# Merged row loads, sums and output stores, and tokens stored in pieces, in an attention kernel with a SwiGLU gate

## Chip, cores and metric

The kernel runs on one core of a Trainium2 chip. The metric is device time in microseconds (us): 1722.99 us, the median of 3 runs (1722.92 to 1723.66). Five engines work side by side, each through its own list of instructions in order: TensorE (PE) for matrix products, VectorE (DVE), ScalarE (ACT), GpSimd (POOL), and SyncE (SP), which here only issues transfers (DMAs). ACT issues a few transfers too. Products land in PSUM, where this kernel has seven banks for them and one for the accumulated attention output.

## What is computed

For 2048 tokens of width 512, in float32:

```python
xn = layernorm(x)
q, k, v = split(xn @ wqkv)          # 32 heads of width 16
p = softmax(q @ k.T * 16 ** -0.5)   # per head, 2048 x 2048
s = (p @ v) @ wo
g = silu((silu(xn @ w1) * (xn @ w3)) @ w2)   # inner width 1792
return x + s * g
```

## The kernel before

**Precision.** Each operand of a product is split into a high and a low part, and three products (low x high, high x low, high x high) give the result. For the 16 rows of one head's keys and queries the three are done in one product over 48 rows: a tile `ks` holds key rows high, low, high, and a tile `qs` query rows high, high, low, 64 rows apart for the two heads of a pair, with two more rows below for the maxima of the softmax.

**First part** (lines 449 to 682). Tokens are loaded in 16 tiles of 128 (`load_x`), normalized, transposed by PE, and split into `xts[b]`, four blocks of 512 tokens. A list `plan` (line 648) then orders the work in steps. Each step makes one product of 12 matmuls: key rows ("k"), query rows ("q") or values ("v") of one block. Then it issues some matmuls of maxima (`max_unit`, line 411: 128 queries against 512 keys of the first pair of heads, reduced by DVE), transposes more token tiles, and last calls a few functions. Keys, queries and values are stored to DRAM (`qk_d`, `v_d`), since later parts read them in another layout: `keep_rows` (line 616) stores one block of key or query rows from SP in two stores (high and low part); `load_k` and `load_q` (lines 392 and 400) bring the 16 rows of a head back, three loads for each of two heads. `keep_tokens` (line 620) stores a block of split tokens from ACT, two stores of 1 MB, for the gate to read later. `token_values` (line 540) copies a value tile on ACT (line 557), stores it from ACT's queue (line 558), and copies a part of it again (line 559). `max_rows` (line 424) turns the maxima of a phase into two rows in `qs`, stored by four small transfers from SP (line 446). `weights_first` starts the loads and splits of the weights for the main part.

**Main part.** 32 phases, one for each half of the queries of 16 pairs of heads. A string, ORDER_OF_ISSUE, gives PE's order letter by letter: "s" a score matmul (`scores`, line 695), followed by an exponential on ACT (line 698); "m" a maximum matmul of the next phase (line 419); "v" four matmuls of probabilities and values (line 711); "f" a matmul of the gate or of the projection of further keys and queries (line 1012). Small and capital letter stand for the two halves of PE's rows. A timing model in the program decides when the work that is not in the string is issued: row loads (`open_chunk`, line 1272), the weights, and the steps of taking out a phase's output, with 16, 1.5, 9, 16 and 5 us between them (LATER).

**Taking out** (`take_out`, line 714). ACT copies the accumulated output `ot`. Four transfers bring the sums of the exponentials into a tile (line 723), DVE takes the reciprocals, one transfer writes them to DRAM (line 727), four read them back broadcast to the rows (line 730). POOL multiplies and splits the result into `oh` and `ol`, and eight transfers store these (line 747). Later `fetch` (line 1047) reads them for the output projection.

**Rows for later heads.** `projected` (line 800) copies a product on ACT, POOL splits it into `ch` and `c`, and SP stores both (line 815). The buffers are shared with those of the gate: ACT's copy to `g` (line 835) reuses one of the two that `ch` uses.

All transfers of one queue leave in the program's order; a transfer that has to wait holds those behind it.

Of the kernel before, what the change touches and what calls it, by code (L numbers as in the profile page):

```python
# [12 lines left out]
ALU = mybir.AluOpType  # L13
# [138 lines left out]
def kernel(ctx: ExitStack, tc: tile.TileContext, x, wqkv, wo, w1, w3, w2, out):  # L152
# [32 lines left out]
    qk_d = [[dram.tile([P, S], F32R, name=f"qk{b}{s}") for s in range(2)] for b in range(8)]  # L185
    o_d = [[[dram.tile([P, 512], F32R, name=f"o{b}{s}{t}") for t in range(TB)] for s in range(2)] for b in range(KC)]
# [204 lines left out]

    def load_k(p, cols=slice(0, S)):
        t = ks[p % 2]
        for h in range(2):
            r = (p % 4) * 32 + h * DH
            kh, kl = (raw(v)[r:r + DH, cols] for v in qk_d[4 + p // 4])
            for n, src in enumerate((kh, kl, kh)):
                nc.sync.dma_start(raw(t)[64 * h + n * DH:64 * h + (n + 1) * DH, cols], src)

    def load_q(p, half, c=None):  # L400
        t = qs[p % 2]
        c = c or slice(half * 1024, (half + 1) * 1024)
        for h in range(2):
            r = (p % 4) * 32 + h * DH
            qh, ql = (raw(v)[r:r + DH, c] for v in qk_d[p // 4])
            for n, src in enumerate((qh, qh, ql)):
                nc.sync.dma_start(raw(t)[64 * h + n * DH:64 * h + (n + 1) * DH, c], src)
# [16 lines left out]
    def max_rows(p, half):  # L424
# [18 lines left out]
        for h in range(2):  # L443
            for n, v in enumerate((mh, ml)):
                r = 64 * h + KM + n
                nc.sync.dma_start(raw(qs[p % 2])[r:r + 1, c], raw(v)[8 * h:8 * h + 8, :])


    with tc.tile_pool(name="pro", bufs=1) as pro, tc.tile_pool(name="pros", bufs=1) as pros:
# [90 lines left out]
        def token_values(b, i):  # L540
# [16 lines left out]
            nc.scalar.copy(vrow[t % 4][:, :, 0:DH], v)  # L557
            nc.scalar.dma_start(v_d[t], vrow[t % 4].rearrange("p h d -> p (h d)"))
            nc.scalar.copy(vt[0][:, t, :, 0:DH], v[:, 0:GH, :])

        nc.gpsimd.memset(raw(ks[0]), 1.0)
        blank = iter([(raw(t), 0.0) for t in qs] + [(r, 1.0) for r in (raw(ks[1]), rb)])
# [35 lines left out]
        first_rows = max_rows(0, 0)  # L598
# [17 lines left out]
        def keep_rows(b, c):  # L616
            for s, st in enumerate(made_rows.pop((b, c))):
                nc.sync.dma_start(raw(qk_d[KC * c][s])[:, b * 512:(b + 1) * 512], raw(st))

        def keep_tokens(b):  # L620
            for s in range(2):
                nc.scalar.dma_start(raw(xt_d[b][s]), raw(xts[b][s]).rearrange("p k t -> p (k t)"))
# [21 lines left out]
        def weights_first():  # L644
            wts.pump(KC)
            wts.fill()

        plan = [
            ("k", 0, (4, 5), 0, keys_here(0)[:1]),
            ("q", 0, (6,), 0, ()),  # L650
            ("v", 0, (7,), 0, queries_here(0)[:1] + keys_here(0)[1:] + queries_here(0)[1:]),
            ("v", 1, (8,), 0, (lambda: keep_tokens(0),)),
            ("k", 1, (9, 10), 0, ()),
            ("q", 1, (11,), 4, keys_here(1)),
            ("v", 2, (12, 13), 5, queries_here(1) + (lambda: keep_tokens(1),)),
            ("k", 2, (14,), 5, ()),
            ("q", 2, (15,), 5, keys_here(2)),
            ("v", 3, (), 6, queries_here(2)),
            ("v", 0, (), 6, (blank_next,)),
            ("k", 3, (), 6, (lambda: load_q(1, 0), lambda: keep_tokens(2))),  # L660
            ("q", 3, (), 6, keys_here(3)),
            ("v", 1, (), 6, queries_here(3) + (lambda: load_q(0, 1),)),
            ("v", 2, (), 6, (blank_next, blank_next, wts.start)),
            ("v", 3, (), 6, (weights_first,)),
            ("v", 0, (), 3, (lambda: next(first_rows), lambda: next(first_rows))),
            ("v", 1, (), 0, (lambda: next(first_rows), lambda: next(first_rows, None))),
            ("v", 2, (), 0, ()),
            ("v", 3, (), 0, ()),
        ]
        done = 0  # L670
        for what, n, tiles_, maxima_, then in plan:
# [9 lines left out]
            for e in then:  # L681
                e()

# [30 lines left out]
    def take_out(p, half):  # L714
# [7 lines left out]
        for j in range(4):  # L722
            nc.sync.dma_start(sums[32 * j:32 * j + 32, :], ot[32 * j + DH:32 * j + VW, :])
# [9 lines left out]
        oh = work.tile([P, 512], F32R, tag="oh", name="oh", bufs=1)  # L733
        ol = work.tile([P, 512], F32R, tag="ol", name="ol", bufs=1)
        nc.gpsimd.tensor_scalar(oh, ot, 1.0, 1.0, op0=ALU.mult, op1=ALU.mult)
        nc.gpsimd.tensor_sub(ol, ot, raw(oh))
        yield
        store_rows(p, half, oh, ol)

    def store_rows(p, half, oh, ol):  # L740
# [764 lines left out]
```

## Time and profile before

| | |
|---|---|
| median of 3 runs | 1722.99 us |
| the profiled execution | 1721.93 us, its span 1719.8 us |
| PE busy | 1699.1 us (99%) |
| DVE, ACT, POOL busy | 80%, 72%, 51% |
| mean granted PE clock | 0.996 |
| transfers | 181.07 MB, 105 GB/s on average |

The profile is of one execution. A row of the timeline reads: start in us, length in us, engine (with a q for its queue of transfers), line, operation, output tile <- input tiles, shape, count, and in square brackets the engine's idle time before it with what ended that. A row of the windows reads: stretch, its length, the busy time of PE, PEld (weight loads of PE), DVE, ACT and POOL with counts, granted clock, share of the 16 DMA engines that was busy, and GB/s. A row of the chain of waits: start, length, what was waited for. Matmuls are pipelined and their ends are modelled.

### The profile page before, as it was taken

How to read it: one execution, taken by the hardware profiler on the slowest of the kernel's cores; microseconds unless marked ns; L12 is line 12 of the kernel's file. 1: busy time of each engine (PE TensorE's matmuls, PEld its weight loads, DVE VectorE, ACT ScalarE, POOL GpSimd, SP SyncE). 2: the span in 40 equal slices, each digit the busy share in tenths (PEclk: the TensorE clock that was granted, in tenths of full speed). 3: DMA queues.
4: the chain of work that ended last, by engine and by line, in shares of the span. 5: the costliest groups of instructions: out<-in, count | busy, mean ns of one | idle time of the engine just before them, and what ended most of it. 6: DMA issues, size and time to landing. Idle time of an engine off the chain costs nothing.

```text
span 1719.8 us, 35915 instructions
## 1 busy us (share of the span) xinstructions
PE 1699.1 (99%) x13476; PEld 1128.0 (66%) x13476; DVE 1371.2 (80%) x2288; ACT 1232.1 (72%) x2449; POOL 877.9 (51%) x926
## 2 busy tenths in 40 slices
PE   9899999999999999999999999999999999999998
PEld 7566665766666666766676666666666666665466
DVE  5769988987887877888797877888888887788735
ACT  5247777778776777777776777777778777778852
POOL 5545652466445664456446663556366705753001
PEclk9999999999999999999999999999999999999999
DMA  7663442433245333422254442322423322341254
GB/s 249 223 189 92 127 117 69 110 104 78 75 111 135 114 98 108 102 65 57 63 161 105 128 124 82 86 74 57 112 84 75 81 39 61 89 104 32 78 183 169
DMA packets 170892, 181.07 MB, mean 105 GB/s; under 512 B 43872, under 2 KB 115552, under 8 KB 167744
## 3 DMA queue, kind: packets, MB, share of 16 engines
q1 hardware_dynamic: 166688, 166.47, 35.8%
q10 hardware_dynamic: 4032, 12.32, 1.8%
q8 instruction: 106, 1.74, 0.4%
q14 instruction: 66, 0.54, 0.1%
HBM read 131.56 MB, written 46.11 MB: 103 GB/s over the span
## 4 chain that ended last, share of the span: by engine, by line
PE 90%; DMA 3%; issue 2%; POOL 2%; SPq 1%; DVE 1%; ACT 1%; ACTq 0%; POOLq 0%; DVEq 0%
PE f L1012 31%; PE pv L711 26%; PE m L419 15%; PE e L695 15%; PE m L552 2%; DMA xin<-in_A_x_dram 1%; DMA inh<-in_A_x_dram 1%; DMA qs<-qk 1%; DMA qk<-sl 0%; POOL sl L611 0%; PE m L434 0%; DMA last<-in_A_wo_dram 0%; DMA ks<-qk 0%; SPq L747 0%; PE o L201 0%
## 5 line engine op out<-in xcount | busy, mean ns | idle before, releaser
L421 DVE TENSOR_REDUCE mp<-m 128x1 f32<-128x512 f32 x2048 | 1277.6, 684 | 232.3 <-PE m L419 151.6
L698 ACT ACTIVATE pt<-e 128x512 f32<-128x512 f32 x2048 | 1059.4, 613 | 269.8 <-PE e L695 142.3
L419 PE MATMUL m<-ks,qs 62*128 62x512 f32 x2048 | 743.1, 412 | 10.2 <-DMA qs<-qk 4.6
L695 PE MATMUL e<-qs,ks 64*128 64x512 f32 x2048 | 742.4, 407 | 0.0
L711 PE MATMUL pv<-pt,vt 128*17 128x512 f32 x4096 | 479.7, 596 | 0.0
L419 PEld LDWEIGHTS m<-ks,qs 62*128 62x128 f32 x2048 | 351.1, 184 | 120.5 <-issue 38.3
L695 PEld LDWEIGHTS e<-qs,ks 64*128 64x128 f32 x2048 | 351.9, 184 | 105.0 <-issue 34.7
L711 PEld LDWEIGHTS pv<-pt,vt 128*17 128x17 f32 x4096 | 100.8, 97 | 253.4 <-issue 248.9
L1012 PE MATMUL f<-xtl,wh 64*128 64x512 f32 x504 | 183.9, 391 | 0.0
L1012 PE MATMUL f<-xth,wh 64*128 64x512 f32 x504 | 181.3, 392 | 0.0
L1012 PE MATMUL f<-xth,wl 64*128 64x512 f32 x504 | 181.1, 392 | 0.0
L1012 PE MATMUL f<-wh,hs 64*128 64x512 f32 x528 | 167.2, 393 | 0.0
L1012 PE MATMUL f<-xtl,xeh 64*128 64x512 f32 x440 | 160.8, 391 | 0.0
L1012 PE MATMUL f<-xth,xeh 64*128 64x512 f32 x440 | 158.6, 393 | 0.0
L1012 PE MATMUL f<-xth,xel 64*128 64x512 f32 x440 | 157.3, 394 | 0.0
L855 POOL TENSOR_TENSOR h<-g,h 128x512 f32<-128x512 f32 x56 | 72.0, 1287 | 164.1 <-ACT h L851 164.0
L340 POOL TENSOR_TENSOR wl<-wr,wh 128x512 fp32r<-128x512 f32 x105 | 135.3, 1289 | 8.8
L1012 PE MATMUL f<-xeh,hs 64*128 64x512 f32 x368 | 118.5, 394 | 0.4 <-POOL hs L857 0.4
L340 POOL TENSOR_TENSOR xel<-wr,xeh 128x512 fp32r<-128x512 f32 x87 | 112.1, 1289 | 7.3
L339 POOL TENSOR_SCALAR xeh<-wr 128x512 fp32r<-128x512 f32 x87 | 53.8, 618 | 104.4 <-PE m L419 48.6
L1012 PE MATMUL f<-wl,hs 64*128 64x512 f32 x264 | 99.1, 392 | 0.0
L1012 PEld LDWEIGHTS f<-wh,hs 64*128 64x128 f32 x528 | 92.9, 185 | 6.6 <-issue 3.4
(243 smaller groups left out, 2143.8 us busy)
## 6 DMA issues: line engine op xcount, KB each, us to landing
wr<-in_B_w_dram SPq DMA_DIRECT2D x168, 256.0 KB
qs<-qk SPq DMA_DIRECT2D x186, 64.0 KB
ks<-qk SPq DMA_DIRECT2D x90, 128.0 KB
ovh<-xt SPq DMA_DIRECT2D x36, 256.0 KB
ovl<-xt SPq DMA_DIRECT2D x36, 256.0 KB
wr<-in_A_wqkv_dram SPq DMA_DIRECT2D x30, 256.0 KB
qk<-ch SPq DMA_DIRECT2D x24, 256.0 KB
qk<-c SPq DMA_DIRECT2D x24, 256.0 KB
```

Source lines behind the costliest of these rows:

```text
L339: nc.gpsimd.tensor_scalar(hi, t, 1.0, 1.0, op0=ALU.mult, op1=ALU.mult)
L340: nc.gpsimd.tensor_sub(lo, t, raw(hi))
L419: nc.tensor.matmul(ps, qs[p % 2][64 * h:64 * h + KM, q0:q0 + P], ks[p % 2][64 * h:64 * h + KM, c * 512:(c + 1) * 512], start=True, stop=True)
L421: nc.vector.reduce_max(mp[p, half][:, h, qt, c:c + 1], ps, axis=AX.X)
L552: nc.tensor.matmul(ps, lhs, wv[k][h == 1], start=n == 0, stop=n == len(three) - 1)
L695: nc.tensor.matmul(ps, ks[p % 2][64 * h:64 * h + KR, k * P:(k + 1) * P], qs[p % 2][64 * h:64 * h + KR, q0:q0 + 512], start=True, stop=True)
L698: done = nc.scalar.activation(pt, ps, AF.Exp, scale=DH ** -0.5)
L711: nc.tensor.matmul(pv[32 * j:32 * j + VW, :], vt[2 * p // GH][:, key, 2 * p % GH + j % 2, :], pt, start=key < 2 if last else k == 0, stop= ...
L855: nc.gpsimd.tensor_mul(h2, g, h2)
L1012: nc.tensor.matmul(ps, left[r], right[r], start=starts and lane == 0, stop=ends and lane == 1)
```

## The change

- Key and query rows: high and low part are in one DRAM tile, and one load brings both into two neighbouring groups of 16 rows; a second load brings the part that is needed twice. Keys now lie low, high, high. Four loads instead of six.
- Sums: one load instead of four. Reciprocals: one broadcast load to all 128 rows instead of four to 16 rows each. Outputs: high and low part in one tile, four stores instead of eight (the last pair's outputs, which stay on the chip, keep eight).
- First part: tokens are stored in 24 pieces of 256 KB from SP, one or two after each step of the plan, instead of six stores from ACT. The store of a value tile comes after the second copy, and those of the first block come together two steps later. Key rows of the first block are loaded ahead of the query stores. Two counts of maxima change (6 to 5, 3 to 4). Half of the first maximum rows go out from ACT's queue. One memset on POOL goes.

Cut to its core:

```diff
-    qk_d = [[dram.tile([P, S], F32R, name=f"qk{b}{s}") for s in range(2)] for b in range(8)]
-    o_d = [[[dram.tile([P, 512], F32R, name=f"o{b}{s}{t}") for t in range(TB)] for s in range(2)] for b in range(KC)]
+    qk_d = [dram.tile([2, P, S], F32R, name=f"qk{b}") for b in range(8)]
+    o_d = [[dram.tile([P, 2, 512], F32R, name=f"o{b}{t}") for t in range(TB)] for b in range(KC)]
...
+    def rows_in(t, two, src, r, h, cols):
+
+        both = raw(src)[:, r:r + DH, cols]
+        at = 64 * h + two * DH
+        nc.sync.dma_start(raw(t)[at:at + 2 * DH, cols], both)
+        at = 64 * h + 2 * (1 - two) * DH
+        nc.sync.dma_start(raw(t)[at:at + DH, cols], both[1 - two])
+
     def load_k(p, cols=slice(0, S)):
-        t = ks[p % 2]
         for h in range(2):
-            r = (p % 4) * 32 + h * DH
-            kh, kl = (raw(v)[r:r + DH, cols] for v in qk_d[4 + p // 4])
-            for n, src in enumerate((kh, kl, kh)):
-                nc.sync.dma_start(raw(t)[64 * h + n * DH:64 * h + (n + 1) * DH, cols], src)
+            rows_in(ks[p % 2], 0, qk_d[4 + p // 4], (p % 4) * 32 + h * DH, h, cols)
...
-    def max_rows(p, half):
+    def max_rows(p, half, queues=(nc.sync, nc.sync)):
...
-                nc.sync.dma_start(raw(qs[p % 2])[r:r + 1, c], raw(v)[8 * h:8 * h + 8, :])
+                queues[h].dma_start(raw(qs[p % 2])[r:r + 1, c], raw(v)[8 * h:8 * h + 8, :])
...
             nc.scalar.copy(vrow[t % 4][:, :, 0:DH], v)
+            nc.scalar.copy(vt[0][:, t, :, 0:DH], v[:, 0:GH, :])
+            if b:
+                store_values(t)
+
+        def store_values(t):
             nc.scalar.dma_start(v_d[t], vrow[t % 4].rearrange("p h d -> p (h d)"))
-            nc.scalar.copy(vt[0][:, t, :, 0:DH], v[:, 0:GH, :])
...
-        def keep_tokens(b):
-            for s in range(2):
-                nc.scalar.dma_start(raw(xt_d[b][s]), raw(xts[b][s]).rearrange("p k t -> p (k t)"))
+        stored_tokens = iter([(b, s, k) for b in range(TB - 1) for s in range(2) for k in range(KC)])
+
+        def keep_tokens(n):
+            for _ in range(n):
+                b, s, k = next(stored_tokens)
+                nc.sync.dma_start(raw(xt_d[b][s])[:, k * 512:(k + 1) * 512], raw(xts[b][s])[:, k, :])
...
-            ("k", 0, (4, 5), 0, keys_here(0)[:1]),
-            ("q", 0, (6,), 0, ()),
-            ("v", 0, (7,), 0, queries_here(0)[:1] + keys_here(0)[1:] + queries_here(0)[1:]),
-            ("v", 1, (8,), 0, (lambda: keep_tokens(0),)),
-            ("k", 1, (9, 10), 0, ()),
...
-            ("k", 3, (), 6, (lambda: load_q(1, 0), lambda: keep_tokens(2))),
-            ("q", 3, (), 6, keys_here(3)),
-            ("v", 1, (), 6, queries_here(3) + (lambda: load_q(0, 1),)),
-            ("v", 2, (), 6, (blank_next, blank_next, wts.start)),
-            ("v", 3, (), 6, (weights_first,)),
-            ("v", 0, (), 3, (lambda: next(first_rows), lambda: next(first_rows))),
...
+            ("k", 0, (4, 5), 0, 0, keys_here(0)),
+            ("q", 0, (6,), 0, 0, (values_first,)),
+            ("v", 0, (7,), 0, 0, queries_here(0)),
+            ("v", 1, (8,), 0, 1, ()),
+            ("k", 1, (9, 10), 0, 2, ()),
...
+            ("k", 3, (), 6, 1, (lambda: load_q(1, 0),)),
+            ("q", 3, (), 6, 2, keys_here(3)),
+            ("v", 1, (), 5, 2, queries_here(3) + (lambda: load_q(0, 1),)),
+            ("v", 2, (), 6, 2, (blank_next, wts.start)),
+            ("v", 3, (), 6, 2, (weights_first,)),
+            ("v", 0, (), 4, 0, (lambda: next(first_rows), lambda: next(first_rows))),
...
-        for j in range(4):
-            nc.sync.dma_start(sums[32 * j:32 * j + 32, :], ot[32 * j + DH:32 * j + VW, :])
+        nc.sync.dma_start(sums, ot[DH:P:32, :])
...
-        for j in range(4):
-            nc.sync.dma_start(rb[32 * j:32 * j + DH, :], rd[j:j + 1, :].to_broadcast([DH, 512]))
+        nc.sync.dma_start(rb, rd.rearrange("j (o c) -> j o c", o=1).to_broadcast([4, 32, 512]))
...
-                for s, v in enumerate((oh, ol)):
-                    b = half * 2 + qb
-                    dst = raw(o_d[p // 4][s][b]) if p < NP - 1 else raw(ov[b][s][p // 4])
-                    nc.sync.dma_start(dst[r:r + DH, :], raw(v)[j:j + DH, :])
+                b = half * 2 + qb
+                if p < NP - 1:
+                    nc.sync.dma_start(raw(o_d[p // 4][b])[r:r + DH], raw(o2)[j:j + DH])
+                    continue
+                for s in range(2):
+                    nc.sync.dma_start(raw(ov[b][s][p // 4])[r:r + DH, :], raw(o2)[j:j + DH, s, :])
```

`load_q` changes as `load_k` does; `values_first` stores the four value tiles of the first block; the fifth entry of a step of the plan is the number of token pieces stored after it.

More of the change, by code (lines that the diff above doesn't have):

```diff
@@ L669 @@
+            ("v", 1, (), 0, 0, (lambda: next(first_rows), lambda: next(first_rows, None))),
+            ("v", 2, (), 0, 0, ()),
+            ("v", 3, (), 0, 0, ()),
         ]
         done = 0
-        for what, n, tiles_, maxima_, then in plan:
+        for what, n, tiles_, maxima_, pieces_, then in plan:
             if what == "v":
@@ L728, in take_out, with store_rows @@
         yield
-        for j in range(4):
-            nc.sync.dma_start(rb[32 * j:32 * j + DH, :], rd[j:j + 1, :].to_broadcast([DH, 512]))
+        nc.sync.dma_start(rb, rd.rearrange("j (o c) -> j o c", o=1).to_broadcast([4, 32, 512]))
         yield
         nc.gpsimd.tensor_mul(ot, ot, rb)
[L733 to L736, printed above, removed]
+        o2 = work.tile([P, 2, 512], F32R, tag="o2", name="o2", bufs=1)
+        nc.gpsimd.tensor_scalar(o2[:, 0, :], ot, 1.0, 1.0, op0=ALU.mult, op1=ALU.mult)
+        nc.gpsimd.tensor_sub(o2[:, 1, :], ot, raw(o2[:, 0, :]))
         yield
-        store_rows(p, half, oh, ol)
-    def store_rows(p, half, oh, ol):
+        store_rows(p, half, o2)
+    def store_rows(p, half, o2):
         for qb in range(2):
@@ L1219, in projecting @@
             turn_back(ps)
-            oh, ol = (work.tile([P, 512], F32R, tag=f"o{v}", name=f"o{v}", bufs=1) for v in "hl")
+            o2 = work.tile([P, 2, 512], F32R, tag="o2", name="o2", bufs=1)
+            oh, ol = o2[:, 0, :], o2[:, 1, :]
             nc.vector.tensor_mul(ot, ot, ps)
```

40 lines of the change are left out of this document (19 added, 21 removed).

## The prediction

> **What bounds the kernel now.** I read the page first, then a table of windows, then what TensorE (PE) waited for, and only then the timelines around those waits.
>
> ```profile
> span 1719.8 us, 35915 instructions
> ...
> PE 1699.1 (99%) x13476; PEld 1128.0 (66%) x13476; DVE 1371.2 (80%) x2288; ACT 1232.1 (72%) x2449; POOL 877.9 (51%) x926
> ```
>
> PE is busy for all but 1719.8 - 1699.1 = 20.7 us. The change takes nothing from PE, so it can only win time in which PE stands still or runs slowly. The windows say where that is (first number after the stretch: its length; then PE's busy time; the last three: granted clock, DMA share, GB/s).
>
> ```profile
> 40.00:50.00 10.00, 7.86 (x29) 5.62 (x28) 7.18 (x16) 4.37 (x8) 6.22 (x11) 0.83 0.70 267
> ...
> 80.00:90.00 10.00, 6.57 (x19) 4.36 (x19) 4.53 (x8) 0.80 (x2) 1.57 (x2) 0.70 0.43 136
> ...
> 500.00:600.00 100.00, 97.81 (x805) 64.59 (x803) 81.18 (x136) 69.25 (x140) 65.10 (x67) 0.98 0.50 128
> ...
> 900.00:1000.00 100.00, 97.53 (x820) 67.22 (x821) 78.95 (x132) 74.95 (x149) 66.34 (x68) 1.00 0.44 119
> 1000.00:1700.00 700.00, 699.96 (x5609) 450.92 (x5602) 544.83 (x898) 522.55 (x1038) 323.86 (x334) 1.00 0.33 89
> ```
>
> From 1000 to 1700 us PE loses 0.04 us: there is nothing to win. Two stretches of the first part lose most and have a lowered clock; two places of the main part lose about 2 us each. PE's waits name the causes:
>
> ```profile
> PE m L419 <- DMA qs<-qk: 4.6, 2, 2.5
> PE m L419 <- DMA ks<-qk: 3.4, 1, 3.4
> PE m L419 <- ACT g L835: 2.2, 1, 2.2
> ...
> PE m L552 <- ACT vt L559: 1.2, 3, 0.4
> PE m L552 <- ACT xeh L523: 0.9, 1, 0.9
> ```
>
> These are 4.6 + 3.4 + 2.2 + 1.2 + 0.9 = 12.3 us, and all of them end in a transfer or in ScalarE (ACT) work behind one. The chain shows what a wait costs besides, for the same twelve products:
>
> ```profile
> 46.29 4.35 PE m L552 x12
> ...
> 75.55 6.76 DMA qk<-sl
> ...
> 85.54 5.43 PE m L552 x12
> ...
> 96.54 3.02 PE m L552 x12
> ```
>
> At full clock twelve products take 3.02 us; after the wait near 43 us they take 4.35, after the one near 81 us 5.43. So these waits cost 1.33 and 2.41 us more in clock. The Trainium skill (TensorE: Matmul & The Clock Gate, Part 1) lets the clock fall after an idle window of about 3.4 us. By that rule a wait of about 2 us would cost no clock, and the sum below would be 1.3 us smaller. The trace disagrees at the first wait, which is shorter than that (its row follows), so the rows decide.
>
> **The change, part by part.** First, the query loads of the first block.
>
> ```profile
> 36.75 4.88 SPq L407 DMA_DIRECT2D qs<-qk  x6
> ```
> ```profile
> 45.00 0.71 PE L419 MATMUL m<-ks,qs 62*128 62x512 f32 x3 [2.14 <-DMA qs<-qk]
> ```
>
> PE waits 2.14 us for loads that SyncE (SP) issues in 4.88 us, six of them, behind six key loads. The change puts the key loads ahead of the query stores and makes each six into four. At 4.88 / 6 = 0.8 us each that is at least 2 x 0.8 = 1.6 us from the query loads alone, and the key loads no longer stand between the query store and them. The token stores of 1 MB each (128 x 2048 numbers by the code) that ACT issues at this stage become one piece of 256 KB. I count the wait and its clock as gone: 2.14 + 1.33 = 3.47 us.
>
> Second, the last key block.
>
> ```profile
> 73.31 0.39 ACTq L622 DMA_DIRECT2D xt<-ovl  x1
> ```
> ```profile
> 81.72 2.83 SPq L398 DMA_DIRECT2D ks<-qk  x6
> ```
> ```profile
> 10.00:20.00 10.00, 9.12 (x46) 6.77 (x45) 6.12 (x18) 6.15 (x12) 6.02 (x16) 1.00 1.06 368
> ```
>
> The store of the key rows took 6.76 us to land (chain above), because 2 MB of tokens had been put ahead of it at 73.31 us; at 368 GB/s, the rate of a saturated window, 2 MB take 5.7 us. Only then could the key loads start, at 81.72. In pieces of 256 KB, one or two at each step, 0.7 to 1.4 us stand ahead of the store: it lands some 4.3 us earlier. The plan's counts of maxima (6 become 5, a 3 becomes 4) also move the first reader of this block behind one more product of 3.02 us. Together 7.3 us against a wait of 3.4: gone, with its clock, 3.43 + 2.41 = 5.84 us.
>
> Third, the value stores behind the second copy on ACT.
>
> ```profile
> 15.67 0.21 ACT L559 COPY vt<-m 128x64 f32<-128x64 f32 x1 [2.08 <-DMA xin<-in_A_x_dram]
> ```
>
> ACT stood 2.08 us before this copy, behind a store that waited for an earlier load; PE's 0.9 us (L523) and the three of 0.4 us (L559) follow from the store's place between the two copies. Gone: 2.1 us. The first four stores come two steps later as one group; nobody reads them in this part, and ACT, busy for 72% on the page, has room for four issues. If they waited again, ACT's next copy would be late by what is left of the 2.08 us.
>
> The sum of the first part is 3.47 + 5.84 + 2.1 = 11.4 us. What comes up next? The second key block has less room once 4 us before it are gone. Two loads of half a block (16 rows of 2 KB each) carry 64 KB; at a single engine's 368 / 1.06 / 16 = 21.7 GB/s a sequence of 16 rows takes 1.5 us. I set 0 to 1.5 us, and take 0.7: 10.7 us remain. The 24 token pieces cost SP 24 issues of about 0.4 us (as the store at 73.31), spread over thirteen steps of some 4 us; SP's idle time hides them, and without it the next row store would leave 0.8 us later. The two first maximum rows that ACT's queue now issues have 24 products as cover. The memset of the reciprocals' tile that goes is POOL's alone.
>
> Now the main part. What is merged, by the table of DMA issues:
>
> ```profile
> qs<-qk SPq DMA_DIRECT2D x186, 64.0 KB
> ks<-qk SPq DMA_DIRECT2D x90, 128.0 KB
> ...
> o<-oh SPq DMA_DIRECT2D x120, 32.0 KB
> o<-ol SPq DMA_DIRECT2D x120, 32.0 KB
> ...
> rb<-rd SPq DMA_DIRECT2D x116, 32.0 KB
> ...
> sums<-ot SPq DMA_DIRECT2D x116, 2.0 KB
> ```
>
> Row loads fall by a third (276 to 184 here), output stores from 240 to 120, sums and reciprocals from 116 to 29 each: some 390 issues fewer, of 0.4 to 0.8 us each. All of it is SP time that PE does not feel, except where a reader already waits. There are two such places.
>
> ```profile
> 916.17 2.76 SPq L398 DMA_DIRECT2D ks<-qk  x6
> ```
> ```profile
> 924.61 0.47 PE L419 MATMUL m<-ks,qs 62*128 62x512 f32 x1 [2.47 <-DMA qs<-qk]
> ```
>
> The key load of the ninth pair of heads was issued at 916.17, behind eight output stores and four loads of sums, and PE stood from 922.14 to 924.61.
>
> ```profile
> 524.06 3.08 SPq L723 DMA_DIRECT2D sums<-ot  x4
> 527.18 0.58 SPq L815 DMA_DIRECT2D qk<-ch  x1
> ```
> ```profile
> 529.64 0.59 ACT L835 COPY g<-f 128x512 f32<-128x512 f32 x1 [3.89 <-DMA qk<-ch]
> ```
>
> Here a store of projected rows left only at 527.18, behind the same dozen, and ACT waited 3.89 us for its buffer, PE 2.2 us. Four sums cost 0.77 us each, so one alone saves 2.3 us, and four stores fewer, at 0.4 each, save 1.6: both places start about 3.9 us earlier. The merged store must wait for both halves of an output; SP's second store waits for the second half already, and everything behind it on SP with it, so this adds nothing. The keys' wait goes: 2.5 us. The other place would go with its clock, 2.2 + 1.3 = 3.5 us, if transfers stay as quick as now.
>
> That is the open price. The merged row load has an outermost step that counts two parts; no transfer of this trace has that shape. From below: it spreads like the loads now, and costs nothing. From above: it runs on two engines only, one part each, so that 16 rows of 8 KB follow each other on one engine.
>
> ```profile
> 915.00:927.00 12.00, 9.53 (x82) 8.49 (x80) 8.66 (x14) 8.69 (x17) 9.02 (x10) 1.00 0.84 166
> ```
>
> At 21.7 GB/s these 131 KB take 6.0 us for a half of the heads; at the 166 / 0.84 / 16 = 12.4 GB/s of the window with that key load, 10.6 us. With 1.9 us for issue and start the keys would land 7.9 or 12.5 us after the issue. The reader above wanted them at 922.14, and an issue at 912.3 leaves 9.8 us. I take 7.9 us, since with only two engines writing there is less to share than in that window, and then the keys' 2.5 us are still won. But both halves and the queries behind them (16 rows of 4 KB, half as long) keep those engines occupied for 2 x 6 + 2 x 3 = 18 us, and anything spread over all engines lands behind them. So I count 2 of the 3.5 us at 527, and a loss where a store meets such a stretch:
>
> ```profile
> 1016.46 2.96 SPq L398 DMA_DIRECT2D ks<-qk  x6
> ...
> 1026.07 0.38 SPq L815 DMA_DIRECT2D qk<-ch  x1
> ```
>
> This store leaves 9.6 us after the key loads begin; 18 us of queue make it 8 us late instead of 2, and ACT waits as at 527, 3.9 us or a little more. Price for PE: 2.2 + 1.3 = 3.5 us; I take 3. The main part: -2.5 - 2 + 3 = -1.5 us (from -6.0 with all engines to +5 with another such store).
>
> The Trainium skill (DMA: Bandwidth & Descriptors, on why a DMA increments its semaphore by 16) has a rule that speaks against this merge: a copy uses the largest number of engines up to 16 that divides the slowest dimension of both sides, thus two for these loads and four for the merged sums and reciprocals. By that rule the upper price holds; without it the sum would be 16.7 to 17.4 us of gain. No run here shows it yet.
>
> For sums and reciprocals the same bounds run from nothing to a transfer of 256 KB on four engines, 64 KB each, 3 us; the code leaves 16 us after each, so neither end counts.
>
> Sum: 10.7 + 1.5 = 12.2 us. The profiled execution took 1721.93 us, 2.1 more than its span, so 1709.7; it lies 1.06 below the median of the runs, 1722.99, from which I forecast 1722.99 - 12.2 = 1710.8, rounded 1711.
>
> **The rivals.** (A) Slower: two-engine loads miss their readers. It decides where a half's rows need more than 9.8 us, that is where an engine moves less than 131 KB in 7.9 us, 16.6 GB/s; the window above (12.4) speaks for it, the saturated one (21.7) against. The wait is then 12.5 - 9.8 = 2.7 us with 1.3 to 2.4 of clock, some 4.5 us. All of 15 key loads would cost 68; the trace has one wait in 15, so I price six: 27 - 11.4 = 15.6 slower, 1739. (B) The weights of the main part become the bound.
>
> ```profile
> 93.14 0.62 POOL L339 TENSOR_SCALAR xeh<-wr 128x512 fp32r<-128x512 f32 x1 [11.56 <-DMA wr<-in_A_wqkv_dram]
> ```
> ```profile
> 108.71 0.50 PE L1012 MATMUL f<-xth,xel 64*128 64x512 f32 x1
> ```
>
> PE wants them at 108.71, about 97 when 11.4 us are gone. POOL splits the first from 93.14 to about 95.1, and its loads stand on SP behind query loads; held up by two engines for 6 us they would be ready at 101: 4 us and 1.3 of clock back, 1716. (C) The waits of the first part only move to the next blocks: two waits of 2.1 us, each with 1.3 to 2.4 of clock, give back 8 of 10.7, and the main part gains nothing: 1720, no measurable change. (D) The loads keep all engines: 11.4 + 6.0 = 17.4, 1705.5.
>
> **How the numbers follow.** Forecast 0.50, A 0.12, B 0.14, C 0.10, D 0.14. The range reaches from just below D, 1704.5, to 1721, which leaves out A and a little of either end. About 0.2%, 3.4 us, is what a measurement of this kernel can tell from no change, so faster means below 1719.5: forecast, B, D and a fifth of C, 0.80. Same: the rest of C, 0.08. Slower: A, 0.12.
>
> **What would show it.** In the changed profile PE has no wait over 1 us between 40 and 90 us and full clock there; the first product of L1012 starts near 97 us (at 108.7 I am wrong in the first part). PE waits no longer for key rows near 910 us. If the loads run on two engines, the six-fold issues shrink to four, but the last of them lands 12 us or more after the first issue, and ACT's copy to g waits longest for the row store that now leaves at 1026.07. Many waits of PE for key rows after 200 us would prove A.

## The result, and the profile after

The changed kernel took 1731.71 us (median of 4 runs, 1731.0 to 1736.07), the kernel before 1722.95 in the same comparison (1719.34 to 1723.66). The ratio is 1.006, 95% interval 1.0039 to 1.0082: slower by 0.6%, where I had forecast 1711 us. All times below are of fast runs; one slow run of 9424 us, of the kernel with the value stores later, is left out. The profiled execution of the changed kernel took 1731.00 us with a span of 1729.2. The page of the profile:

```profile
span 1729.2 us, 35378 instructions
...
PE 1698.3 (98%) x13476; PEld 1128.3 (65%) x13476; DVE 1370.7 (79%) x2288; ACT 1230.9 (71%) x2449; POOL 878.9 (51%) x925
```

PE does the same work; it is busy for all but 30.9 us, where it was 20.7. 537 instructions are gone and 10.2 us of idle time have come. The windows, the same ones as before (length, then PE's busy time; last the granted clock, DMA share, GB/s):

```profile
40.00:50.00 10.00, 7.81 (x38) 5.21 (x37) 9.48 (x21) 4.52 (x9) 6.44 (x11) 1.00 0.58 211
80.00:90.00 10.00, 4.32 (x18) 2.65 (x14) 3.22 (x7) 1.19 (x4) 0.41 (x1) 0.81 0.47 166
500.00:600.00 100.00, 94.43 (x768) 63.53 (x766) 77.82 (x130) 69.07 (x139) 63.00 (x65) 0.97 0.43 119
900.00:1000.00 100.00, 99.11 (x831) 67.70 (x829) 80.35 (x135) 74.42 (x148) 68.93 (x71) 1.00 0.48 136
```

80 to 90 us loses 5.7 us (3.4 before), 500 to 600 loses 5.6 (2.2 before); 900 to 1000 is better by 1.6. What PE waited for:

```profile
PE m L422 <- ACT g L849: 8.2, 3, 5.6
PE m L422 <- DMA ks<-qk: 7.5, 3, 5.5
PE m L422 <- DVE mp L424: 2.2, 1, 2.2
PE m L422 <- DMA qs<-qk: 1.9, 1, 1.9
PE e L710 <- DMA qs<-ml: 1.3, 1, 1.3
...
PE e L201 <- ACT xth L526: 1.1, 1, 1.1
```

The waits for queries fell from 4.6 to 1.9 us, those for ACT's vt copies are gone. The waits for keys grew from 3.4 to 7.5 and those for the ACT copy g from 2.2 to 8.2; three kinds of over 1 us are new. To see where the time was lost I set the same product of both traces side by side. The first product of the main part (L1026; before it was L1012, at 108.71) stands here:

```profile
110.33 0.50 PE L1026 MATMUL f<-xth,xel 64*128 64x512 f32 x1
...
112.40 0.47 PE L710 MATMUL e<-qs,ks 64*128 64x512 f32 x1 [1.33 <-DMA qs<-ml]
```

So the first part, forecast to end near 97, ends 1.6 us later than before, and the first attention product 3.2 later (112.40 against 109.21). Counting on by the 2048 products for row maxima, the delay is 4.7 us behind the wait at 150 us (1.4 us for ACT g), 8.6 behind the one at 532 (5.6 us), 10.7 behind the one at 740 (1.3 us), and 9.1 behind 933, where the wait for keys is 0.9 us in place of 2.5. It ends at 9.3, against 9.4 us between the two spans.

**The first loss.** The chain of the changed kernel around 80 us (start, length, what):

```profile
77.63 7.26 DMA qk<-sl
...
86.72 4.11 DMA ks<-qk
...
92.59 4.71 PE m L555 x12
```

The store of the last key rows, which I had expected to land some 4 us earlier than before, takes 7.26 us where it took 6.76. The key loads start at 84.94, 3.2 us later than before (81.72), and PE stands 5.54 + 1.11 us. No token store of 2 MB is ahead of the store any more; ahead of it on SyncE (SP) stand four loads of query rows, two of them merged.

The landing events, the marks that a transfer leaves on its completion semaphore, tell how this store is late. It leaves 16 of them: 14 come within 3.4 us of its issue, the last two at 6.81 and 7.26. A store of values that ACT issued from its own queue at 80.40 looks the same: 14 within 2.3 us, the last two at 4.72 and 4.93. So two shares of sixteen are late, and not those of SP's transfers alone.

**The second loss.** SP's timeline, and ACT's row that waits, around 530 us:

```profile
512.39 0.65 SPq L396 DMA_DIRECT2D ks<-qk  x1
...
516.55 7.57 SPq L396 DMA_DIRECT2D qs<-qk  x1
...
528.24 4.16 SPq L758 DMA_DIRECT2D o<-o  x4
532.50 0.62 SPq L737 DMA_DIRECT2D sums<-ot  x1
534.80 0.34 SPq L829 DMA_DIRECT2D qk<-ch  x1
```
```profile
537.50 0.59 ACT L849 COPY g<-f 128x512 f32<-128x512 f32 x1 [7.26 <-DMA qk<-ch]
```

The key block's loads begin at 512.39; SP then stands 7.57 us at one issue, and the store of projected rows, which ACT's copy needs out of its buffer, leaves at 534.80 where it left at 527.18. From 526.05 to 527.71 SP stands once more, until the key load issued at 513.61 has landed. (That load is eight transfers ahead, on the same completion semaphore; more of this under the value stores.) The store itself lands 2.62 us after its issue, so here it is SP that is late, and not the store on its way. What the DMA engines do meanwhile (the changed kernel):

```profile
520.00:522.00 2.00, 2.00 (x22) 1.43 (x16) 1.17 (x3) 1.04 (x3) 1.92 (x3) 1.00 0.12 49
522.00:524.00 2.00, 2.00 (x21) 1.88 (x18) 1.99 (x4) 2.00 (x6) 0.05 (x1) 1.00 0.14 57
```

A DMA share of 0.12 to 0.14 is about two of sixteen engines (0.125), at 25 GB/s each (49 / (0.12 x 16), 57 / (0.14 x 16)). The same stage in the kernel before:

```profile
512.00:514.00 2.00, 2.00 (x20) 0.78 (x12) 0.91 (x3) 0.91 (x2) 1.91 (x3) 1.00 1.03 131
...
518.00:520.00 2.00, 2.00 (x21) 1.88 (x19) 1.99 (x4) 2.00 (x6) 1.39 (x2) 1.00 1.03 178
```

There all engines are busy. So the merged row loads run on two engines by these figures, and the other fourteen stand nearly idle meanwhile. That is what the trace says; whether it is the cause of both losses was for the experiments.

### The profile page after: what moved, and what is told of

Read it like the earlier page. It is cut to its first block, busy times and chain, and to the rows that moved or that the text cites. A ratio compares the mean times of both kernels' runs of the same rounds, so it can differ in the third digit from the quotient of the medians.

```text
span 1729.2 us, 35378 instructions
## 1 busy us (share of the span) xinstructions
PE 1698.3 (98%) x13476; PEld 1128.3 (65%) x13476; DVE 1370.7 (79%) x2288; ACT 1230.9 (71%) x2449; POOL 878.9 (51%) x925
## 4 chain that ended last, share of the span: by engine, by line
PE 89%; DMA 5%; issue 2%; SPq 1%; POOL 1%; DVE 1%; ACT 1%; ACTq 0%; POOLq 0%; DVEq 0%
PE f L1026 31%; PE pv L726 26%; PE m L422 15%; PE e L710 15%; PE m L555 1%; DMA ks<-qk 1%; DMA qk<-sl 1%; DMA qs<-qk 1%; SPq L396 1%; DMA inh<-in_A_x_dram 1%; PE o L201 0%; PE m L437 0%; DMA ovh<-o 0%; PE o L203 0%; PE o L205 0%
## 5 line engine op out<-in xcount | busy, mean ns | idle before, releaser
L1026 PE MATMUL f<-xtl,wh 64*128 64x512 f32 x504 | 184.0, 391 | 0.0
L1026 PE MATMUL f<-xth,wh 64*128 64x512 f32 x504 | 181.3, 392 | 0.0
L1026 PE MATMUL f<-xth,wl 64*128 64x512 f32 x504 | 181.1, 392 | 0.0
L1026 PE MATMUL f<-wh,hs 64*128 64x512 f32 x528 | 167.1, 393 | 0.0
L1026 PE MATMUL f<-xtl,xeh 64*128 64x512 f32 x440 | 161.0, 391 | 0.0
L1026 PE MATMUL f<-xth,xeh 64*128 64x512 f32 x440 | 158.4, 392 | 0.0
L1026 PE MATMUL f<-xth,xel 64*128 64x512 f32 x440 | 157.5, 395 | 0.0
L1026 PE MATMUL f<-xeh,hs 64*128 64x512 f32 x368 | 118.7, 394 | 0.4 <-POOL hs L871 0.4
L1026 PE MATMUL f<-wl,hs 64*128 64x512 f32 x264 | 99.0, 392 | 0.0
L339 POOL TENSOR_SCALAR wh<-wr 128x512 fp32r<-128x512 f32 x105 | 65.3, 622 | 63.6 <-PE e L710 42.1
```

The source lines that it names most:

```text
L339: nc.gpsimd.tensor_scalar(hi, t, 1.0, 1.0, op0=ALU.mult, op1=ALU.mult)
L1026: nc.tensor.matmul(ps, left[r], right[r], start=starts and lane == 0, stop=ends and lane == 1)
```

## The experiments

The outermost step of a load is the slowest one of its access pattern: a merged load of the change steps over the two parts first, and over 16 rows inside each. Theory T: a load whose outermost step counts two runs on two engines, and what follows on SP's queue lands late. Rivals: R1, the token pieces, now in SP's queue, make the store at 77.63 late whatever the loads' shape; R2, the merged sums and reciprocals cost the main part its waits; R3, not the count of the outermost step but the distance of the two parts, or the load of 32 rows as such, is slow. All kernels were timed in five rounds, in three sets of four; the kernel before took 1720.2, 1720.5 and 1720.0 us (medians) in these sets.

### Loads apart (changed kernel, row loads undone)

```
     def rows_in(t, two, src, r, h, cols):
         both = raw(src)[:, r:r + DH, cols]
-        at = 64 * h + two * DH
-        nc.sync.dma_start(raw(t)[at:at + 2 * DH, cols], both)
-        at = 64 * h + 2 * (1 - two) * DH
-        nc.sync.dma_start(raw(t)[at:at + DH, cols], both[1 - two])
+        for n, part in enumerate((0, 0, 1) if two else (0, 1, 1)):
+            at = 64 * h + n * DH
+            nc.sync.dma_start(raw(t)[at:at + DH, cols], both[part])
```

> The changed kernel (1731.7 us) with one thing undone: every row load is again three loads of 16 rows; sums, reciprocals, outputs and the whole first part stay as changed. Theory T (a load of two parts runs on two DMA engines, and everything behind it on SyncE's queue lands late): the waits for keys near 83 us (6.65 us) and for ACT g near 150, 532 and 740 us (8.2 us) go or fall below 2.2 us, the wait near 47 us for VectorE (2.2) stays; time 1712 to 1717 us. Rival R1 (the token pieces in SyncE's queue make the row store of the last key block late, whatever the loads' shape): TensorE still waits over 4 us for that block near 83 us, and the time stays above 1722. Rival R2 (the merged sums and reciprocals on four engines): the waits for ACT g in the main part stay, over 5 us in all, time 1718 to 1724.

Measured 1714.09 us; ratio to before 0.9965 (0.9952 to 0.9979). PE's longest waits now:

```profile
PE m L421 <- DMA ks<-qk: 5.7, 3, 2.9
PE e L709 <- DMA qs<-ml: 2.7, 1, 2.7
```

All three waits for ACT g are gone, so R2 falls for those. The store of the last key rows, with all token pieces in SP's queue, lands 3.03 us after its issue in place of 7.26, so R1 falls too. The wait of 2.2 us for VectorE, which I had expected to stay, went as well. For the last key block PE still waits 1.69 + 2.91 us, less than with two engines but more than T had it: something of that wait isn't the shape (see the value stores below).

### Merged loads alone, on two engines (kernel before plus rows_in)

```
-    qk_d = [[dram.tile([P, S], F32R, name=f"qk{b}{s}") for s in range(2)] for b in range(8)]
+    qk_d = [dram.tile([2, P, S], F32R, name=f"qk{b}") for b in range(8)]
...
-                nc.sync.dma_start(raw(t)[64 * h + n * DH:64 * h + (n + 1) * DH, cols], src)
+            rows_in(ks[p % 2], 0, qk_d[4 + p // 4], (p % 4) * 32 + h * DH, h, cols)
```

> The kernel before (1723.0 us) with one thing added: row loads merged as in the change; nothing else. Theory T: the main part shows the same late landings as the changed kernel (key loads around 9 us at the median where they took 4.2) and one or more waits for ACT g; the first part has loads of 2 KB rows at two engines as well, so its waits do not shrink; slower than before by 5 to 13 us, 1728 to 1736. Rivals R1 and R2: the loads are not the cause, so within 2 us of before, 1721 to 1725.

Measured 1748.06 us; ratio 1.0163 (1.0149 to 1.0176): 28 us slower, more than twice what I expected. PE's waits:

```profile
PE m L422 <- ACT g L838: 10.3, 2, 9.1
PE m L422 <- DMA ks<-qk: 10.1, 3, 5.1
PE m L422 <- DMA qs<-qk: 8.4, 3, 3.6
```

The loads alone make all three kinds of wait that changed. The rest of the change gives back more than half of their price.

### Rows in pairs (same transfers, 32 rows outermost)

```
-    qk_d = [dram.tile([2, P, S], F32R, name=f"qk{b}") for b in range(8)]
+    qk_d = [dram.tile([P, 2, S], F32R, name=f"qk{b}") for b in range(8)]
...
+        both = raw(src)[r:r + DH, :, cols]
+        nc.sync.dma_start(raw(t)[at:at + 2 * DH, cols], both.rearrange("r p c -> (r p) c"))
+        nc.sync.dma_start(raw(t)[at + 2 * DH:at + 3 * DH, cols], both[:, single])
```

> The changed kernel with the same number of transfers and the same bytes, but the two parts of a row stored side by side in DRAM, so that a merged load's outermost step counts 32 rows in place of two parts (the 48 rows of keys and queries stand in another order, the same for both). Theory T: the merged loads spread like single ones, land in 4 to 7 us, and the time is that of the kernel with the loads apart or up to 3 us less, 1710 to 1716. If it is the merging itself that costs (fewer transfers in flight, a longer one in front), it stays within 3 us of the changed kernel, 1729 to 1735. R1: above 1722 with the wait near 83 us.

Measured 1702.37 us; ratio 0.9898 (0.9884 to 0.9911). It beats both kernels. PE's waits are down to these:

```profile
PE e L709 <- DMA qs<-ml: 1.5, 1, 1.5
...
PE m L421 <- DVE mp L423: 0.8, 1, 0.8
```

The token pieces are all still in SP's queue and no wait for keys is left, which speaks against R1 again.

### The first part alone (kernel before plus pieces, plan, value stores)

The diff is that of the change without rows_in, the merged sums, reciprocals and output stores. (DRAM tiles and the order of the key rows stay as changed.)

> The kernel before with the first part's changes alone (token pieces on SyncE, value stores behind the second copy, the new plan); loads, sums, reciprocals and output stores are all as many as before. Theory T: the first part gains most of what was forecast, less the 2.2 us that TensorE now waits for VectorE near 47 us and about 1 us near 34 us: 6 to 9 us, and the main part is as before: 1714 to 1717. Rival R1: the last key block still waits over 4 us near 83 us and the first part gains less than 2 us: 1721 to 1727.

Measured 1719.01 us; ratio 0.9991 (0.9982 to 1.0), so next to nothing in the whole time. That is 2 us above T's range and 2 below R1's. Yet the first product of the main part starts at 102.95, 5.8 us earlier than before. PE's waits say what took it back:

```profile
PE m L421 <- DMA ks<-qk: 5.4, 3, 2.8
PE e L709 <- DMA qs<-ml: 1.9, 1, 1.9
PE m L421 <- DVE mp L423: 1.6, 2, 1.0
```

The keys of the last block are still waited for (1.72 + 2.79 us, nearly as with the loads apart), although the store of their rows lands 3.02 us after its issue. And a new wait, for the first row of maxima (ml), stands at the seam to the main part with 3.4 us at half clock behind it; 128 row maxima on, 2.2 us of the gain are left. Against the kernel with the loads apart, which has the merged sums, reciprocals and outputs besides, it is 4.9 us slower.

### Steps swapped (the sharpest one)

```
-        nc.sync.dma_start(raw(t)[at:at + 2 * DH, cols], both)
+        nc.sync.dma_start(raw(t)[at:at + 2 * DH, cols], both.rearrange("p (a b) c -> a p b c", a=16))
```

(The single row load goes to the last 16 of the 48 rows for keys and queries both, so that the order agrees.)

> The changed kernel with the DRAM layout, the transfers and the bytes as they are, and only the steps of a merged load swapped: it reads row 0 of both parts, then row 1 of both, so its outermost step counts 16 rows with 2 parts inside, where the change has 2 parts with 16 rows inside. Theory T (the count of the outermost step is the number of DMA engines): as good as the rows stored in pairs, 1700 to 1706, key loads landing in 4 to 7 us. Rival R3 (it is the distance of the two parts in DRAM, 1 MB, or the load of 32 rows as such): no better than the changed kernel, 1728 to 1735.

Measured 1704.87 us; ratio 0.9904 (0.9891 to 0.9918): DRAM layout, transfers and bytes of the changed kernel, and 24 us less when each median is set against the kernel before of its own comparison (8.8 above, 15.6 below), 27 by the ratios. R3 falls. The same windows again, to set beside those of the changed kernel:

```profile
40.00:50.00 10.00, 9.91 (x51) 6.91 (x51) 8.55 (x18) 5.36 (x11) 7.30 (x12) 1.00 0.62 221
80.00:90.00 10.00, 9.26 (x44) 6.10 (x42) 7.93 (x13) 1.73 (x5) 0.00 (x0) 1.00 0.60 207
500.00:600.00 100.00, 100.00 (x843) 66.40 (x843) 83.22 (x139) 73.38 (x147) 62.09 (x64) 1.00 0.52 134
```

80 to 90 us loses 0.7 us in place of 5.7, and 500 to 600 us nothing. The loads of the same key block on SP and the store behind them:

```profile
498.55 0.61 SPq L396 DMA_DIRECT2D ks<-qk  x1
...
503.32 0.55 SPq L396 DMA_DIRECT2D qs<-qk  x1
...
510.91 0.49 SPq L828 DMA_DIRECT2D qk<-ch  x1
```

From the first key load to the store it takes 12.4 us; in the changed kernel it took 534.80 - 512.39 = 22.4, of which 7.57 were the one stand. The kernel with merged loads alone on two engines has the same stand, 7.01 us at 522.45; with the steps swapped no row load has one.

### Eight and four engines

One unused row of DRAM behind every four (every eight) keeps the source from being one even run of rows:

```
-    qk_d = [dram.tile([P, 2, S], F32R, name=f"qk{b}") for b in range(8)]
+    qk_d = [dram.tile([2 * P // 4, 5, S], F32R, name=f"qk{b}") for b in range(8)]
...
+        both = raw(src)[2 * r // 4:2 * r // 4 + 8, 0:4, cols]
```

> The kernel with the rows in pairs, but with one unused row in DRAM after every four, so that the outermost step of every row load (the single ones too) counts 8. Theory T: eight engines, 2 rows of 8 KB on each fewer than half of the price of the change: key loads land in 4 to 8 us and no wait above 1.5 us appears that the pairs did not have: 1701 to 1707. If two steps instead of one in the source is what costs: above 1720.

> As the kernel with eight, with one unused row after every eight, so that the outermost step of all row loads counts 4. Theory T: four engines carry 65 KB (merged) and 33 KB (single) each for half of a key block, 4 us at the 24 GB/s at which one engine worked in the changed kernel, against 5.4 us there: half to three quarters of the price comes back; key loads land in 6 to 11 us and the store near 530 us is late again: 1706 to 1722. If the price has a threshold between 2 and 4 engines it stays within 3 us of the pairs.

Measured 1710.49 us (ratio 0.9938, 0.9925 to 0.995) with eight, 1717.13 (0.9979, 0.9969 to 0.9988) with four. The eight missed my range by 3.5 us, and my bound on its waits: PE waits three times for keys, 5.3 us in all and 2.0 at the longest. Beside them, from the landing events in the traces, the time from issue to landing of the 38 merged key loads (30 of a half of a key block, 8 short ones of the first part) and the number of events that mark one landing. The times come from different comparisons, so the ratio to the kernel before stands with them:

| outermost count | events | landing, median / 90th percentile | time, us (ratio) |
|---|---|---|---|
| 2 (changed kernel) | 3 | 9.4 / 13.9 us | 1731.7 (1.006) |
| 4 | 5 | 5.8 / 8.9 | 1717.1 (0.9979) |
| 8 | 9 | 4.9 / 6.9 | 1710.5 (0.9938) |
| 16 (steps swapped) | 16 | 4.6 / 6.5 | 1704.9 (0.9904) |
| 32 (pairs) | 16 | 4.2 / 6.7 | 1702.4 (0.9898) |

No threshold shows: the price falls with every doubling up to 16, most at the first; the intervals don't tell 16 from 32. (At four and eight the single loads of 16 rows are limited as well, so these two prices are a little too high for the merged loads by themselves.) At four the wait for ACT g is still there, at eight it isn't:

```profile
PE m L422 <- DMA ks<-qk: 3.9, 2, 3.2
...
PE m L422 <- ACT g L849: 1.4, 1, 1.4
```

The rule of the Trainium skill that the prediction cited (DMA: Bandwidth & Descriptors, "Why a DMA increments its semaphore by 16 and not by 1") says two engines for the changed kernel's load and sixteen for the swapped one; the traces agree, with shares of 0.12 to 0.14 and with the table.

### Sums and reciprocals apart, with pairs and with two engines

```
-        nc.sync.dma_start(sums, ot[DH:P:32, :])
+        for j in range(4):
+            nc.sync.dma_start(sums[32 * j:32 * j + 32, :], ot[32 * j + DH:32 * j + VW, :])
```

and the same for rb.

> The kernel with the rows in pairs, with sums and reciprocals again as four transfers each. Theory T says that a merged sum or reciprocal on four engines is neither gain nor loss for TensorE by itself, but that fewer issues on SyncE free the places near 527 and 916: with the loads on 16 engines those places may come back in part: 1702 to 1706. If the merged reciprocals (landing in 5.9 us where they took 2.0) were a cost, it would fall below 1701.

> The changed kernel with sums and reciprocals again as four transfers each on 16 engines; row loads stay on two. Rival R2 (four-engine sums and reciprocals cost in the main part): the waits for ACT g of 8.2 us shrink, 1724 to 1729. Theory T: the two-engine loads alone do it; the 174 issues more on SyncE make the same waits as long or longer: 1731 to 1740.

With the rows in pairs: 1704.51 us (ratio 0.9904, 0.989 to 0.9918), which the intervals don't tell from 1702.37. With two-engine loads: 1741.72 (1.0124, 1.0109 to 1.014), 10 us slower than the changed kernel (their intervals lie apart) and above the top of T's range. PE's waits in the latter:

```profile
PE m L422 <- DMA ks<-qk: 14.1, 5, 4.6
PE m L422 <- ACT g L851: 7.6, 2, 6.7
```

So R2 is wrong in its sign where the row loads run on two engines: there merged sums and reciprocals help, although a reciprocal lands in 6.0 us at the median where it took 2.0 (five landing events, as the loads on four engines leave). With 16 engines no difference is told. That it is the smaller number of issues that helps was not tested by itself.

### Value stores later (what was left with the loads apart)

The chain of the kernel with the loads apart explains its 1.69 + 2.91 us:

```profile
79.75 2.15 DMA v<-vrow
...
81.92 0.30 SPq L397
...
82.26 1.81 DMA ks<-qk
...
84.16 1.39 PE m L421 x5
```

A key load waits for a store of values, which nobody reads here. The transfers of SP and ACT share eight completion semaphores in turn, so each one waits for the one eight places ahead of it, and the fifth of six key loads came eight behind this store.

```
-            if b:
+            if b and t not in (9, 10):
                 store_values(t)
...
-            ("v", 3, (), 6, 2, (weights_first,)),
+            ("v", 3, (), 6, 2, (weights_first, lambda: store_values(9), lambda: store_values(10))),
```

> The kernel with the loads apart (1714.1 us), with two value stores (the tenth and eleventh) issued after the four steps they stand in instead of right behind their copies. There SyncE's fifth key load of the last block stood from 79.4 to 81.9 us behind such a value store (the chain goes product, ACT copy, value store 2.15 us, SyncE, key load 1.81 us, product), and TensorE waited 1.69 + 2.91 us. Theory V (the wait that is left with 16 engines comes from that value store): both waits together fall below 1.5 us and the half clock behind them goes: 1707 to 1711. Rival: six loads at 0.5 to 0.9 us of SyncE each are simply too many behind the row store; the waits stay above 3 us and the time within 1.5 us of 1714.

Measured 1711.14 us, the median of five runs; ratio 0.9945 (0.9932 to 0.9958), against 0.9965 with the loads apart. These intervals overlap, so the trace has to tell. The two waits are 1.07 + 0.88 = 1.95 us in place of 4.60, and the 3.4 us at half clock behind them are gone; my 1.5 was too low. Some of it is lost again at the seam:

```profile
PE e L709 <- DMA qs<-ml: 3.4, 1, 3.4
```

The wait for the row of maxima grew from 2.7 to 3.4 us. The value store was the cause of more than half of what was left.

### The first maximum rows on SP

```
-        first_rows = max_rows(0, 0, (nc.sync, nc.scalar))
+        first_rows = max_rows(0, 0)
```

> The kernel with the rows in pairs (1702.4 us) with the first maximum rows all on SyncE, as before the change. There TensorE waits 1.51 us near 96 us for a row that ACT could issue only behind a value store of 4.9 us. If ACT's queue is what makes it late: the wait goes, 1700 to 1702. If SyncE's queue, with weight loads of 5.8 to 6.5 us in it, is as late: 1702 to 1706.

Measured 1706.03 us; ratio 0.9914 (0.9901 to 0.9927). The wait is longer, not gone:

```profile
PE e L709 <- DMA qs<-ml: 3.2, 1, 3.2
```

It was 1.5 in the kernel with pairs, with no half clock behind it; here 3.4 us at half clock follow. So SP's queue is no earlier than ACT's, and giving two rows to ACT's is a small gain of the change. It rests on the trace: the intervals of the two times overlap.

### Pairs alone on the kernel before

> The kernel before (1720 us in these runs) with the merged row loads alone, rows stored in pairs so that they run on 16 engines: the partner of the run that added them on two engines (1748). Theory T: 184 loads in place of 276 and nothing slower; the waits for queries near 43 us and for keys near 81 and 922 us shrink: 1710 to 1718. If merging is worth nothing by itself and only the first part's plan gains: 1719 to 1722.

Measured 1715.53 us; ratio 0.9973 (0.9964 to 0.9982). This kernel differs from the one of 1748.06 us in the order of a load's steps and of the rows, in DRAM and in the tiles, alone: 32 us lie in that. Merging on 16 engines is worth 4.5 us by itself; here the waits at 79 us (4.17 us) and at 526 (1.26) are still there.

## Why the prediction was wrong

**The step that failed** is the price of the merged row load, and above all the list of who pays it. I had both ends, all engines or two, with the shape of the load and the rule named, and it failed in both parts of the sum.

In the first part I priced two-engine loads at "0 to 1.5 us", by the time that one of them takes by itself. The seam to the main part came 3.2 us later than before, not 10.7 earlier: 13.9 us missed. With the steps swapped, and nothing else, it comes 9.1 us earlier, so the shape cost 12.3 of these.

In the main part I chose "7.9 us" to land, "less to share than in that window". The 30 loads of a half of a key block landed in 10.2 us at the median, the one issued at 512.39 in 9.9, by the landing events. That alone was a size. The larger error was the next sentence: I let one store pay ("I take 3", at 1026), although I had worked out a queue of 18 us behind every key block. That store did land late, 11.2 us after its issue at 1026.87, much as I had it. But ACT's copy to g starts at 1038.15 without a wait, for ACT was busy until then, and PE waits for nothing there. The store at 527, where I counted 2 us of gain, stood behind just such a queue, and it cost 5.57 us of wait in place of 2.19. The places at 150 and 740 us, which I had not looked at, had no wait before and lost 3.6 us together (delay 4.7 - 3.2 and 10.7 - 8.6). So the main part lost 9.3 - 3.2 = 6.1 us where I had forecast a gain of 1.5.

Its own sign came as well: the first product of L1026 stands at 110.33, past the 108.7 at which I had called the first part wrong.

**Query loads of the first block, 3.47 us forecast.** Right as far as it went: the wait at 42.86 us and its clock went, and the first part's product matmul that started at 49.3 started at 45.5 (the 81st of 192). But 2.19 us for VectorE (47.29) and 1.87 us for the next queries (58.65) took it back. That is rival C on a small scale. With the rows in pairs both are gone; with the steps swapped 0.82 us of the second is left.

**Last key block, 5.84 us forecast.** Wrong by more than its size. Two merged query loads stood ahead of the store of the key rows; they land 6.2 and 7.4 us after their issue, and the store behind them takes 7.26. I had forgotten who comes behind them. The pieces do what I said they do: with the loads apart the same store lands 3.0 us after its issue. The wait went for good only with fewer loads on all engines (pairs, steps swapped), since six loads also met the value store.

**Value stores, 2.1 us forecast.** The three waits for the vt copies (1.2 us) are gone, and of the 0.9 us for xeh 0.3 is left. "If they waited again, ACT's next copy would be late" came true:

```profile
33.73 0.59 ACT L560 COPY vrow<-m 128x512 f32<-128x512 f32 x1 [4.59 <-DMA ks<-qk]
```

ACT stood 4.59 us behind the group of value stores, for a key load, and PE 1.12 at 34 us. With pairs that is gone too.

**The two maximum rows "have 24 products as cover".** They had not: PE waited 1.33 us for one.

**Sums and reciprocals, "neither end counts".** Right where the loads run on all engines (1702.4 and 1704.5, not told apart), wrong where they don't: 10 us.

**Keys of the ninth pair, 2.5 us forecast.** 0.9 us of wait were left where 2.5 were: a gain of 1.6.

**The rivals.** A named the right resource and the right sign, but not the right victims, nor the size (1739): it let key rows miss their readers six times in the main part and kept the whole gain of the first part. In the main part keys were waited for once, 0.9 us; ACT's copies behind late stores were waited for three times, and the first part's gain was lost. B did not come: no run has a wait of PE for the weights of the main part. D, all engines, 17.4 us less (that is 1705.6, not 1705.5): the swapped steps give 1704.9 against 1720.5, 15.6 less, and the pairs 17.8. The seam comes 9.1 and 11.7 us earlier in these two (forecast 11.4), so the rest, 6.5 and 6.1 us, is the main part's (forecast 6.0). So the two sums held once the loads ran on 16 engines. Their terms do not stand alone, though: the first part by itself gave 1.2 us in the whole time, merging by itself 4.5, and not 17.8 together.

Why a store behind two busy engines is late, the landing events answer in part. In the first part it is its own two shares on the busy engines, since ACT's value store at 80.40, in the other queue, is late in the same way. In the main part, at 534.80, it is SP, which stands 7.57 us at one issue and then waits for a key load eight transfers ahead. What stays open is what SP waits for in these 7.57 us: the trace names no semaphore.

## What to carry to other kernels

Before two transfers are merged, look at the count of the outermost step: here [2 parts][16 rows] against [16 rows][2 parts] was 24 to 27 us in one kernel and nothing else differed in bytes or number. Price a slow transfer by all that comes behind it, on its engines from either queue and on its issuing engine, at every place where it is issued and not at the worst one. And a DMA share near 2/16 in a window where a queue is full is the sign of it.

## What the runs showed of the hardware that I had not expected

The clock lowered by a wait doesn't follow the wait's length. In the kernel with swapped steps PE waits 0.82 us at 55.27 us (it is idle for 1.07 us in all from 53.5 to 56.95), and half the clock follows from 56.95 to 60.36:

```profile
56.00:60.00 4.00, 3.90 (x13) 3.09 (x14) 1.76 (x3) 0.59 (x1) 3.10 (x4) 0.62 0.96 346
```

In the kernel before, the 2.47 us at 922.14 cost no clock, and in the changed kernel the 2.19 us at 47.29 cost none:

```profile
49.30:53.00 3.70, 3.52 (x19) 2.90 (x20) 1.35 (x3) 2.43 (x4) 1.67 (x2) 1.00 0.78 288
```

(The third number from the right is the granted clock: 0.62 and 1.00.) The stretches at half clock that follow a wait last 3.4, 6.8 or 10.2 us in all these runs, and within a run their starts lie whole multiples of 3.413 us apart (in the kernel before 46.44, 83.98 and 531.13: 11 and 131 steps). The Trainium skill (TensorE: Matmul & The Clock Gate, Part 1) has an idle window of about 3.4 us; the length of the stretches agrees with that step, the 0.82 us don't agree with it as a threshold. So my 1.3 to 2.4 us of clock for each wait were right for some and nothing for others.

A transfer can wait for one that it has nothing to do with, eight places ahead on the shared semaphores: moving two value stores behind the key loads took 2.65 us of PE's waits away (4.60 to 1.95).

A transfer of 16 shares is as late as its slowest two: the store at 77.63 had 14 landing events within 3.4 us and the last at 7.26, and ACT's store at 80.40, in the other queue, 14 within 2.3 us and the last at 4.93.
